# Attention and expert layer on one core: query rows repeated by zero-step DRAM reads, and batch 0's queries cut 512 + 288 + 288, the last two among the expert work

## The chip, the cores and the metric

The kernel runs on one core of one Trainium2 chip. The metric is the device time of one execution in microseconds (us), the median of the runs. A profile of one more execution gives the trace: every instruction of every engine with its start and duration, what it waited for, and the DMA packets. The engines are TensorE (PE; its weight loads have a row of their own, PEld), VectorE (DVE), ScalarE (ACT), GpSimd (POOL) and SyncE (SP), which here only issues DMA transfers. Each runs its own instructions in order and waits for others by semaphores.

## The reference, cut to what matters

```python
# attention: q, k, v are (4, 4, 1088, 32); S1, S2 are (8, 32), float64
def phi(x):                                   # 64 features of a row
    a = np.einsum('rd,bhsd->bhsr', S1, x)
    b = np.einsum('rd,bhsd->bhsr', S2, x)
    return np.einsum('bhsi,bhsj->bhsij', a, b).reshape(*x.shape[:-1], 64)
q_p, k_p = phi(q), phi(k)
kv = np.einsum('bhsf,bhsd->bhfd', k_p, v)
z = np.sum(k_p, axis=2)
x = num / den       # num = q_p kv, den = q_p z + 1e-6; then (4352, 128)

# routed experts: w_gate (128, 8), w1 (8, 128, 1024), w2 (8, 1024, 128)
P = np.exp(x @ w_gate - max)                  # then 8 rounds of row and
out = 0                                       # column normalisation
for e in range(8):
    out += P[:, e:e+1] * (np.maximum(x @ w1[e], 0) @ w2[e])
```

## The kernel before, in words

All arithmetic is in 32-bit floats. Nearly all of the time is the experts' two matrix products. They are cut into *steps* of a generator, `steps()`: one step is the first product of 128 hidden units with one tile of tokens (`first`, L894, two matmuls of 64 output rows each, side by side in the array), its ReLU on ScalarE (L898), and those second products (`into`, L1067) and VectorE sums (L911, L956) that have come due. `fill(n)` runs about `n` / share steps, where a step of 256 tokens counts as 0.53. The attention is written as short pieces with `fill` between them, so that TensorE has expert work while VectorE and ScalarE prepare the next piece. The order on PE and DVE, and in the opening part on ACT too, is the order of the program; the issuing order of DMA transfers and of GpSimd's work is left to a scheduler.

The experts without a weight (`groups`, the first ones of expert 0) need only `xT`, the attention's result transposed, so they can begin when the first tokens of batch 0 are done. PSUM has eight banks: four of the tag `a`, handed out in turn by `bank()`, for everything that is read soon, and four (`s0` to `s3`) for the experts' sums. A new use of a bank waits until its last reader is done.

Batch 0 goes a way of its own, because nothing can hide it:

- 15 matmuls on a tile of ones (L114) run while the first loads arrive. `projections` turns the float64 S1 and S2 to 32 bits and writes the block weights `wd` (one block a head).
- `transpose_k`, `keys_ab` (L304): keys turned, and their two projections `a` and `b` made for all heads.
- `keys_products` (L320), `keys_sums` (L336), `keys_kept`: products a_i b_j of the keys, their sums with v, and the copy of these to `kvz`.
- `query_products(c)` (L366) for three chunks of queries: 384, 352 and 352. The weights `wq` hold each row of S1 and S2 repeated, so that one matmul gives a_i for all 64 pairs (i, j) of two heads and the other gives b_j; the contraction is over the 64 rows of two heads, and the two head pairs run side by side as row tiles. The results lie in `s0` to `s3`. ScalarE copies the a part (L369), `multiply` (L375) forms the product on VectorE.
- `fractions(c)` (L384) makes numerators and denominators, `divide(c)` (L396 to L403) turns the denominators, takes reciprocals, turns them back and writes `xT`.

Batches 1 to 3 make a and b once (`queries_ab`, L419, weights `wdq`), store them to DRAM and read them back with each row repeated over partitions: `qa` is stored with every element twice and read in four transfers to `ph` (`repeat_a`, L435), `qb` is stored eightfold and read in one transfer to `rb` (`repeat_b`, L438). VectorE multiplies `ph` by `rb` in thirds (`times`, L445), `tops` (L454) forms numerators and denominators, `over` (L467 to L473) divides. `take_over` sends the result through DRAM to `xT`. `attention(b)` holds these pieces, with a `fill(1.4)` after each.

Of the kernel before, what the change touches and what calls it, by code (L numbers as in the profile page):

```python
# [10 lines left out]
F32 = mybir.dt.float32  # L11
U32 = mybir.dt.uint32
Act = mybir.ActivationFunctionType
Alu = mybir.AluOpType
# [36 lines left out]
def kernel(  # L51
# [49 lines left out]
    for n, (s, queue) in enumerate(((S1, nc.sync), (S2, nc.scalar))):  # L101
        queue.dma_start(out=raw[:, n], in_=s.bitcast(U32).unsqueeze(0).to_broadcast([P // R, R, words * D]))
# [10 lines left out]
    for _ in range(15):  # L113
        nc.tensor.matmul(warm[:, 0:P], ones, ones, start=True, stop=True)  # L114
# [49 lines left out]
    def load_q(b):  # L164
        qx = ld.tile([P, SA, D], F32, tag="q", name="qx")
        nc.sync.dma_start(out=qx, in_=q[b].rearrange("h (s a) d -> (h s) a d", a=SA))
        loaded["q", b] = qx
# [13 lines left out]
    load_q(0)  # L181
    load_v(0)
    load_q(1)

# [65 lines left out]
    wdq = consts.tile([P, 2, H * R], F32, name="wdq")  # L250
# [10 lines left out]
    def repeated(st):  # L261
        for s in range(2):
            one = half[:, s:s + 1].unsqueeze(2).to_broadcast([P, R, R])
            nc.vector.tensor_tensor(wq[:, 0, s], st[:, 0, 0:R].unsqueeze(2).to_broadcast([P, R, R]), one, op=Alu.mult)
            nc.vector.tensor_tensor(wq[:, 1, s], st[:, 1, 0:R].unsqueeze(1).to_broadcast([P, R, R]), one,
                                    op=Alu.mult)


        nc.gpsimd.tensor_copy(wdq[:, 0], wd[:, 0].rearrange("p h r -> p (h r)"))
        nc.gpsimd.tensor_copy(wdq[:, 1].rearrange("p (r h) -> p r h", h=H), wd[:, 1].rearrange("p h r -> p r h"))  # L270
# [11 lines left out]
    load_v(1)  # L282
# [8 lines left out]
    def transpose_k(b):  # L291
        kx = loaded["k", b]
        nc.vector.transpose(out=kT[:, 0:NT * P].rearrange("p (t c s) -> p c t s", c=4, s=32),  # L293
                            in_=kx[:, 0:4 * NT, :].rearrange("p (c t) d -> p c t d", c=4))
        nc.vector.transpose(out=kT[:, NT * P:S], in_=kx[:, 4 * NT:SA, :].rearrange("p a d -> p (a d)"))

    def keys_ab(b):

        ab = wk.tile([P, 2, NT + 1, H * R], F32, tag="ab", name="ab", bufs=1)
        pk = bank().rearrange("p (t n f) -> p t n f", t=NT, n=2)  # L300
        for t in range(NT):
            for s in range(2):
                sl = slice(64 * s, 64 * (s + 1))
                nc.tensor.matmul(pk[sl, t].rearrange("p n f -> p (n f)"), kT[:, P * t + 64 * s:P * t + 64 * (s + 1)],  # L304
                                 wdf, start=True, stop=True, tile_position=(0, 64 * s))
        nc.scalar.copy(ab[:, :, 0:NT, :], pk.rearrange("p t n f -> p n t f"))
        pr = bank()[0:64, 0:2 * H * R]
        nc.tensor.matmul(pr, kT[:, NT * P:S], wdf, start=True, stop=True, tile_position=(0, 0))
        nc.scalar.copy(ab[0:64, :, NT, :], pr.rearrange("p (n f) -> p n f", n=2))
        keys[b] = ab  # L310
# [32 lines left out]
    def keys_kept(b):  # L343
        pv = sums_of.pop(b)
        for s in range(2):
            sl = slice(64 * s, 64 * (s + 1))
            if b:
                x, y = kvs[b % 2][sl, :, s, :], pv[sl].rearrange("p i c d -> p i (c d)")[:, :, 0:D + 1]
            else:
                x, y = kvz[sl, :, :, s, :], pv[sl].rearrange("p i c d -> p c i d")  # L350
            if s:
                nc.vector.tensor_copy(x, y)
            else:
                nc.scalar.copy(x, y)

    chunks = ((0, 384), (384, 736), (736, S))

    def query_products(c):

        lo, hi = chunks[c]  # L360
        n = hi - lo
        banks = [[mps.tile([P, 512], F32, tag=f"s{2 * i + m}", name="s") for m in range(2)] for i in range(2)]
        for m in range(2):
            for i in range(2):
                sl = slice(64 * i, 64 * (i + 1))
                nc.tensor.matmul(banks[i][m][:, 0:n], wqf[sl, m, :], qT[sl, lo:hi], start=True, stop=True,  # L366
                                 tile_position=(64 * i, 0))
        for i in range(2):
            nc.scalar.copy(phs[0][:, i, lo:hi], banks[i][0][:, 0:n])  # L369
        queries[0, c] = [banks[i][1][:, 0:n] for i in range(2)]  # L370

    def multiply(c):
        lo, hi = chunks[c]
        for i, pb in enumerate(queries[0, c]):
            nc.vector.tensor_tensor(phs[0][:, i, lo:hi], phs[0][:, i, lo:hi], pb, op=Alu.mult)  # L375

    def fractions(c):

        lo, hi = chunks[c]
        n = hi - lo  # L380
        pn, pd = bank(), bank()
        for t, m in ((pd, 1), (pn, 0)):
            for i in range(2):
                nc.tensor.matmul(t[64 * i:64 * (i + 1), 0:n], kvz[:, m, i].rearrange("p h d -> p (h d)"),  # L384
                                 phs[0][:, i, lo:hi], start=True, stop=True, tile_position=(0, 64 * i))
        queries[0, c] = pn, pd

    def divide(c):


        lo, hi = chunks[c]
        n = hi - lo
        nb = n // 32
        pn, pd = queries.pop((0, c))
        rd = wk.tile([P, 384], F32, tag="rd", name="rd")
        nc.vector.transpose(out=rd[:, 0:n], in_=pd[:, 0:n])  # L396
        rc = wk.tile([P, 12], F32, tag="rc", name="rc")[:, 0:nb]
        nc.vector.tensor_scalar_add(rc, rd[:, 0:n].rearrange("p (b r) -> p b r", r=32)[:, :, 0], 1e-6)
        nc.vector.reciprocal(rc, rc)
        rd = wk.tile([P, 384], F32, tag="rd", name="rd")  # L400
        nc.vector.transpose(out=rd[:, 0:n].rearrange("p (b r) -> p b r", r=32),
                            in_=rc.unsqueeze(2).to_broadcast([P, nb, 32]))
        nc.vector.tensor_tensor(xT[:, lo:hi], pn[:, 0:n], rd[:, 0:n], op=Alu.mult)  # L403
# [6 lines left out]
    def queries_ab(b):  # L410
        qa = dram.tile([H * R, 2, 2, 2 * W9], F32, name=f"qa{b}")
        qb = dram.tile([2, R, 2 * R, 2, 2 * W9], F32, name=f"qb{b}")
        ab = wk.tile([P, 3, 192], F32, tag="qab", name="qab", bufs=1)
        x = (kT if b == 1 else qT).rearrange("p (h q c t s) -> p h c t q s", h=2, q=2, c=3, t=3)
        for cs in ((0, 1), (2,)):
            pq = bank()[:, 0:192 * len(cs)].rearrange("p (c n) -> p c n", n=192)
            for i, c in enumerate(cs):
                for s in range(2):
                    nc.tensor.matmul(pq[64 * s:64 * (s + 1), i].rearrange("p (t q s) -> p t q s", t=3, q=2),  # L419
                                     wdq.rearrange("p n f -> p (n f)"), x[:, s, c], start=True, stop=True,  # L420
                                     tile_position=(0, 64 * s))
            nc.scalar.copy(ab[:, cs[0]:cs[-1] + 1], pq)
        abf = ab.rearrange("p c n -> p (c n)")
        for s in range(2):
            x = abf[64 * s:64 * s + 32].unsqueeze(1).to_broadcast([32, 2, 2 * W9])
            nc.sync.dma_start(out=qa[:, :, s], in_=x)
        for s in range(2):
            for h in range(2):
                x = abf[64 * s + 32 + h:64 * (s + 1):2].unsqueeze(1).to_broadcast([2 * R, R, 2 * W9])
                nc.sync.dma_start(out=qb[h, :, :, s].rearrange("i f n -> f i n"), in_=x)  # L430
        queries[b] = qa, qb

    def repeat_a(b):
        for j in range(4):
            nc.sync.dma_start(out=phs[b % 2][j::4], in_=queries[b][0].rearrange("(x r) j s n -> (r j) x (s n)", x=2))  # L435

    def repeat_b(b):
        nc.sync.dma_start(out=rb, in_=queries.pop(b)[1].rearrange("h i (j x) s n -> (h i j) x (s n)", x=2))  # L438
# [25 lines left out]
    def over(b, c):  # L464
        pn = queries.pop((b, c))
        rc = wk.tile([P, 12], F32, tag="rc", name="rc").rearrange("p (t h) -> p t h", h=H)
        nc.vector.reciprocal(rc, pn[:, :, :, D])  # L467
        xs = wk.tile([P, 384], F32, tag="rd", name="rd").rearrange("p (h t d) -> p h t d", h=H, t=3)
# [671 lines left out]
    with tc.manual_schedule(engines={engines.DVE, engines.PE, engines.Activation}):  # L1140
        st = projections()
        transpose_k(0)
        keys_ab(0)
        repeated(st)
        load_k(1)
        transpose_q(0, 0, chunks[0][1])
        query_products(0)
# [3 lines left out]
        multiply(0)  # L1151
        transpose_q(0, chunks[0][1])
        keys_kept(0)
        transpose_q(1)
        query_products(1)
        fractions(0)
        multiply(1)
        queries_ab(1)
        load_q(2)
# [3 lines left out]
        fractions(1)  # L1163
        query_products(2)
        divide(1)
    with tc.manual_schedule(engines={engines.DVE, engines.PE}):
        fill(1)
        multiply(2)
        fractions(2)
        fill(1)  # L1170
        transpose_k(1)
        load_k(2)
        load_v(2)
        load_q(3)
        divide(2)
        fill(1.5)
        keys_ab(1)
        fill(1)
        keys_products(1, 0)
        fill(1)  # L1180
        keys_products(1, 1)
        fill(1)
        keys_products(1, 2)
        fill(1)
# [41 lines left out]
```

## Time and profile before

| | |
|---|---|
| time, median of 3 runs | 932.12 us (931.32 to 932.35) |
| span of the profiled execution | 929.5 us |
| TensorE matmuls busy | 915.1 us, 98% |
| VectorE busy | 696.7 us, 75% |
| ScalarE busy | 417.5 us, 45% |
| GpSimd busy | 204.3 us, 22% |
| DMA | 128.14 MB, 138 GB/s in the mean |

The page gives for each engine its busy time, then a row of 40 equal slices of the span (23 us each), in which a digit is the busy share in tenths. A line of the order of time gives the start, the duration, the engine, the line of the kernel, the operation, its output and inputs, the number of merged instructions, and in brackets the idle time before it with what ended it. A 32-bit matmul appears as two records (two passes). A busy TensorE is one that has matmuls under way, not one at its peak.

### The profile page before, as it was taken

The numbers are of one execution on the slowest core, as the hardware profiler recorded it, in microseconds if no ns is written. First come the engines' busy times: TensorE is split into PE (matmuls) and PEld (weight loads), VectorE is DVE, ScalarE is ACT, GpSimd is POOL, SyncE is SP. The second block draws the span as 40 slices with busy tenths as digits, with TensorE's granted clock in tenths as the row PEclk, the third lists the DMA queues.
The fourth block names the chain that finished last, engine by engine and source line by source line (L and its number), as shares of the span: only waits on it lengthen the run. The fifth ranks groups of instructions, "written<-read, shape, count | busy, mean of one in ns | idle before, by whom it ended". The sixth has DMA issues, their size and how long they took to land.

```text
span 929.5 us, 18877 instructions
## 1 busy us (share of the span) xinstructions
PE 915.1 (98%) x7434; PEld 596.6 (64%) x7434; DVE 696.7 (75%) x1200; ACT 417.5 (45%) x901; POOL 204.3 (22%) x198
## 2 busy tenths in 40 slices
PE   9999999999999999999999999999999999999997
PEld 6667544568888888875555555555555555556886
DVE  8787789896779788686976666965757977768665
ACT  2445345654444454444544444544445444445443
POOL 2021100172545502030020101101110343310220
PEclk9999999999999999999999999999999999999999
DMA  9987100222345535353444434363434555553650
GB/s 229 288 250 218 52 1 1 80 98 63 109 153 170 171 118 155 115 195 118 136 136 143 159 113 143 113 189 125 146 111 154 150 151 184 171 179 91 173 152 12
DMA packets 91640, 128.14 MB, mean 138 GB/s; under 512 B 25376, under 2 KB 69488, under 8 KB 86816
## 3 DMA queue, kind: packets, MB, share of 16 engines
q1 hardware_dynamic: 89344, 123.63, 42.9%
q0 software_dynamic: 976, 3.15, 1.1%
q8 instruction: 58, 0.95, 0.4%
q10 hardware_dynamic: 1232, 0.16, 0.1%
q14 instruction: 30, 0.25, 0.1%
HBM read 107.88 MB, written 19.05 MB: 137 GB/s over the span
## 4 chain that ended last, share of the span: by engine, by line
PE 91%; DVE 6%; issue 1%; ACT 1%; DMA 0%; SPq 0%; POOL 0%; DVEq 0%; ACTq 0%; POOLq 0%
PE a L894 49%; PE s L1067 39%; DVE hb L911 1%; PE a L336 1%; PE a L114 1%; DVE hb L956 1%; PE a L454 1%; DMA ph<-qa 0%; PE a L304 0%; ACT hb L898 0%; DVE cs L593 0%; DVE kp L320 0%; DVE kT L293 0%; DVE pqg L956 0%; PE a L488 0%
## 5 line engine op out<-in xcount | busy, mean ns | idle before, releaser
L894 PE MATMUL a<-xe,w 128*64 128x256 f32 (+1 forms) x2560 | 571.3, 470 | 0.0
L898 ACT ACTIVATE hb<-a 128x256 f32<-128x256 f32 (+4 forms) x408 | 195.3, 480 | 253.4 <-PE a L894 226.3
L894 PEld LDWEIGHTS a<-xe,w 128*64 128x64 f32 x2560 | 242.7, 137 | 76.6 <-issue 1.6
L1067 PE MATMUL s<-hb,ws 128*64 128x256 f32 (+3 forms) x1344 | 267.5, 395 | 1.8 <-DVE w L723 0.9
L898 ACT ACTIVATE hx<-a 128x256 f32<-128x256 f32 (+1 forms) x360 | 167.3, 465 | 214.5 <-PE a L894 194.7
L1067 PE MATMUL s<-hx,ws 128*64 128x256 f32 x1280 | 235.4, 379 | 0.0
L956 DVE TENSOR_TENSOR hb<-hb 128x512 f32<-128x512 f32 (+1 forms) x204 | 133.8, 666 | 95.2 <-ACT hb L898 90.3
L956 DVE TENSOR_TENSOR hx<-hx 128x512 f32<-128x512 f32 (+1 forms) x204 | 148.8, 739 | 68.0 <-ACT hx L898 63.1
L663 POOL TENSOR_TENSOR xe<-xT,xe 128x768 f32<-128x768 f32 (+2 forms) x41 | 84.8, 2070 | 501.7 <-DMA xe<-pT 405.4
L1067 PEld LDWEIGHTS s<-hb,ws 128*64 128x64 f32 x1344 | 127.8, 137 | 92.7 <-issue 63.8
L1067 PEld LDWEIGHTS s<-hx,ws 128*64 128x64 f32 x1280 | 121.2, 137 | 78.7 <-issue 59.4
L894 PE MATMUL a<-xT,w 128*64 128x416 f32 (+3 forms) x512 | 124.4, 464 | 1.3 <-DVE rd L469 0.9
L1067 PE MATMUL s<-hb,w 128*64 128x256 f32 (+3 forms) x496 | 109.6, 410 | 0.5 <-DVE kept L723 0.4
L911 DVE TENSOR_TENSOR hb<-hb 128x416 f32<-128x416 f32 (+7 forms) x96 | 68.1, 711 | 18.2 <-ACT hb L898 12.9
L1067 PE MATMUL s<-hx,w 128*64 128x256 f32 x384 | 76.5, 379 | 0.0
L894 PEld LDWEIGHTS a<-xT,w 128*64 128x64 f32 x512 | 51.8, 137 | 28.7 <-issue 11.8
L1067 PEld LDWEIGHTS s<-hb,w 128*64 128x64 f32 x496 | 50.0, 137 | 23.2 <-issue 6.8
L239 POOL TENSOR_TENSOR ws<-w 128x256 f32<-128x256 f32 (+1 forms) x70 | 59.4, 883 | 12.8 <-PE a L894 9.8
L911 DVE TENSOR_TENSOR hx<-hx 128x256 f32<-128x256 f32 (+1 forms) x65 | 38.8, 602 | 24.6 <-ACT hx L898 20.8
L956 DVE TENSOR_TENSOR pqg<-hb 128x512 f32<-128x512 f32 x68 | 47.5, 739 | 0.0
L1067 PEld LDWEIGHTS s<-hx,w 128*64 128x64 f32 x384 | 38.6, 137 | 8.5
L956 DVE TENSOR_TENSOR pqg<-hx 128x512 f32<-128x512 f32 x68 | 36.4, 574 | 0.0
(170 smaller groups left out, 477.6 us busy)
## 6 DMA issues: line engine op xcount, KB each, us to landing
w<-in_moe_w_dram SPq DMA_DIRECT2D x82, 512.0 KB, 5.6
ws<-ws SPq DMA_DIRECT2D x34, 1024.0 KB, 5.0
xe<-pT SPq DMA_DIRECT2D x34, 384.0 KB, 4.1
ws<-ws SPq DMA_DIRECT2D x12, 512.0 KB, 3.7
qb<-qab SPq DMA_DIRECT2D x12, 288.0 KB, 5.2
ph<-qa SPq DMA_DIRECT2D x12, 288.0 KB, 4.7
rb<-qb SPq DMA_DIRECT2D x3, 1152.0 KB
pb<-pT SPq DMA_DIRECT2D x6, 384.0 KB, 7.4
```

The lines of the kernel that those rows point to most:

```text
L114: nc.tensor.matmul(warm[:, 0:P], ones, ones, start=True, stop=True)
L239: tc.keep_in_program_order(nc.gpsimd.tensor_tensor(ws[:, c:c + len(ns)], blocks(x), blocks(y), op=Alu.subtract if off else Alu.add))
L336: nc.tensor.matmul(pv[64 * s:64 * (s + 1), i], kp[0:n, H * t + h].rearrange("p i j -> p (i j)"), vx[0:n, slots[h], t, :], start=(t == 0 an ...
L454: nc.tensor.matmul(pn[64 * s:64 * (s + 1), t, 2 * i:2 * i + 2].rearrange("p h d -> p (h d)"), ph[:, i, s, 64 * t:64 * (t + 1)], kvs[b % 2] ...
L663: tc.keep_in_program_order(nc.gpsimd.tensor_tensor(out, x, pb, op=Alu.mult))
L894: nc.tensor.matmul(ph[sl], loaded_w[j][0][:, P * f + H2 * s:P * f + H2 * (s + 1)], sources[j][:, lo:hi], start=True, stop=True, tile_posit ...
L898: nc.scalar.activation(out=out, in_=ph, func=Act.Relu)
L911: nc.vector.tensor_tensor(out, a, b, op=Alu.subtract)
L956: nc.vector.tensor_tensor(out if not isinstance(out, tuple) else places(*out), places(*a), places(*b) if isinstance(b, tuple) else b, op=A ...
L1067: nc.tensor.matmul(sums[g][i][H2 * s:H2 * (s + 1), n * place:n * (place + 1)], w, x, start=c == 1, stop=c == per, tile_position=(0, H2 * s))
```

## The change

It has two aims. The first is to move less through DRAM for batches 1 to 3: a and b are stored once, 16 rows by 2304 numbers each, and the repeats are made by the reading side with a step of zero; with that `wdq` isn't needed any more. The half of `rb` for the upper 64 partitions is issued by GpSimd. The second is to let the first expert work begin after one chunk of 512 queries, and to make the products of the other two chunks (288 each) among the expert steps. For that these two use `a` banks and weights `wz`, which hold zeros outside one head and contract over all 128 rows, one matmul a head, side by side as column tiles like the experts' own. Around it: S1 and S2 come by the queues of ScalarE and GpSimd, so that the keys are SyncE's first load; `wq` and `wz` are written by GpSimd; batch 0's keys go in two halves; 14 warming matmuls and not 15; both copies to `kvz` on ScalarE; and the loads and fills in a new order.

```diff
-    for n, (s, queue) in enumerate(((S1, nc.sync), (S2, nc.scalar))):
+    for n, (s, queue) in enumerate(((S1, nc.scalar), (S2, nc.gpsimd))):
...
-    for _ in range(15):
+    for _ in range(14):
...
     load_k(0)
-    load_q(0)
+    load_q(0, 0, 16)
     load_v(0)
     load_q(1)
+    load_q(0, 16)
...
     def repeated(st):
+        def repeat(out, column):
+            one = column.unsqueeze(2).to_broadcast([P, R, R])
+            nc.gpsimd.tensor_tensor(out[:, 0], st[:, 0, 0:R].unsqueeze(2).to_broadcast([P, R, R]), one, op=Alu.mult)
+            nc.gpsimd.tensor_tensor(out[:, 1], st[:, 1, 0:R].unsqueeze(1).to_broadcast([P, R, R]), one, op=Alu.mult)
...
+            repeat(wq[:, :, s], half[:, s:s + 1])
+        for h in range(H):
+            repeat(wz[:, :, h], own[:, h:h + 1])
...
-            if s:
+            if s and b:
                 nc.vector.tensor_copy(x, y)
...
-    chunks = ((0, 384), (384, 736), (736, S))
+    chunks = ((0, 512), (512, 800), (800, S))
...
+        else:
+            banks = {i: [bank(), bank()]}
+            for m in range(2):
+                for s in range(2):
+                    nc.tensor.matmul(banks[i][m][64 * s:64 * (s + 1), 0:n],
+                                     wz[:, m, 2 * i + s].rearrange("p i j -> p (i j)"), qT[:, lo:hi],
+                                     start=True, stop=True, tile_position=(0, 64 * s))
...
     def queries_ab(b):
-        qa = dram.tile([H * R, 2, 2, 2 * W9], F32, name=f"qa{b}")
-        qb = dram.tile([2, R, 2 * R, 2, 2 * W9], F32, name=f"qb{b}")
+        ds = [dram.tile([2 * R, 2, 2, 2 * W9], F32, name=f"q{n}{b}") for n in "ab"]
...
-        for s in range(2):
-            x = abf[64 * s:64 * s + 32].unsqueeze(1).to_broadcast([32, 2, 2 * W9])
-            nc.sync.dma_start(out=qa[:, :, s], in_=x)
-        for s in range(2):
-            for h in range(2):
-                x = abf[64 * s + 32 + h:64 * (s + 1):2].unsqueeze(1).to_broadcast([2 * R, R, 2 * W9])
-                nc.sync.dma_start(out=qb[h, :, :, s].rearrange("i f n -> f i n"), in_=x)
+        for s in range(2):
+            for n, d in enumerate(ds):
+                lo = 64 * s + 32 * n
+                nc.sync.dma_start(out=d[:, :, s].rearrange("r x n -> x r n"), in_=abf[lo:lo + 32])
...
     def repeat_a(b):
-        for j in range(4):
-            nc.sync.dma_start(out=phs[b % 2][j::4], in_=queries[b][0].rearrange("(x r) j s n -> (r j) x (s n)", x=2))
+        rows = queries[b][0].rearrange("r x s n -> r (x s n)")
+        nc.sync.dma_start(out=phs[b % 2], in_=rows.unsqueeze(1).to_broadcast([2 * R, R, 8 * W9]))
     def repeat_b(b):
-        nc.sync.dma_start(out=rb, in_=queries.pop(b)[1].rearrange("h i (j x) s n -> (h i j) x (s n)", x=2))
+        rows = queries.pop(b)[1].rearrange("r x s n -> r (x s n)")
+        for h, queue in enumerate((nc.sync, nc.gpsimd)):
+            queue.dma_start(out=rb[64 * h:64 * (h + 1)],
+                            in_=rows[R * h:R * (h + 1)].unsqueeze(0).to_broadcast([R, R, 8 * W9]))
```

The opening order after the change stands below. Before, the products of all three chunks and two of the three `divide`s stood ahead of the first `fill`, and the fills up to `attention(1)` came to n = 7.5; now they come to 6.25.

```python
projections, repeated, transpose_k(0) in halves, keys_ab(0) in halves
transpose_q(0, 0:512), query_products(0), keys_products(0), keys_sums(0)
multiply(0), keys_kept(0), transpose_q(1), fractions(0, denominators)
queries_ab(1), fractions(0, numerators), repeat_a(1), repeat_b(1)
divide(0), transpose_q(0, 512:1088)
fill(0.5), query_products(1, heads 0 and 1), fill(0.5), multiply
query_products(1, heads 2 and 3), fill(0.5), multiply, fill(0.5)
transpose_k(1), fractions(1), fill(0.5), query_products(2, heads 0 and 1)
divide(1), fill(0.5), multiply, query_products(2, heads 2 and 3)
fill(0.5), multiply, keys_ab(1), fill(0.5), fractions(2)
keys_products(1, 0), fill(0.75), divide(2), keys_products(1, 1), fill(0.75)
keys_products(1, 2), fill(0.75), then attention(1)
```

## The prediction, made before the changed kernel ran

> **What bounds the kernel now.** I read the page's busy rows first, then the waits and the order of time of the first 40 us, where every edit lies.
>
> ```profile
> PE 915.1 (98%) x7434; PEld 596.6 (64%) x7434; DVE 696.7 (75%) x1200; ACT 417.5 (45%) x901; POOL 204.3 (22%) x198
> PE   9999999999999999999999999999999999999997
> DMA  9987100222345535353444434363434555553650
> ```
>
> TensorE (PE) is busy in all 40 slices; the DMA row is full only in the first three. So an edit is worth what it does to TensorE's own work and to its pauses. I split the span that way. One expert step (two matmuls of 256 columns, four records in the trace) takes 0.43 us in the chain of waits wherever it runs freely, that is 0.84 ns for a column of a pair of passes that run side by side. All matmuls at this rate come to 902 us. The other 27 us are lost: 6.9 before the first expert matmul at 20.0, 9.3 by the end of batch 1's key sums at 35.1, about 19 by 110 us, only 2.5 in the 820 us after that, and some 6 at the end. The change can win back a part of the first 19 us and nothing else.
>
> The order of time of the start (start, duration, then the instructions):
>
> ```profile
> 1.00 6.31 PE L114 MATMUL a<-ones 128*128 128x128 f32 x30 [1.00 <-POOL own L116]
> 3.39 0.20 DVE L34 TENSOR_SCALAR mant<-raw 128x64 uint32<-128x64 uint32 x1 [1.64 <-DMA raw<-in_S_dram]
> 7.25 1.15 PE L304 MATMUL a<-wd,kT 128*64 128x64 f32 x32
> 8.49 1.56 PE L366 MATMUL s<-qT,wq 64*128 64x384 f32 x8
> 9.06 2.69 DVE L320 TENSOR_TENSOR kp<-ab 128x1024 f32<-128x1024 f32 x3 [0.63 <-ACT ab L306]
> 10.35 2.66 PE L336 MATMUL a<-v,kp 128*64 128x64 f32 x72 [0.30 <-DVE kp L320]
> 13.65 1.46 PE L366 MATMUL s<-qT,wq 64*128 64x352 f32 x8 [0.64 <-DVE qT L289]
> 15.03 1.51 PE L384 MATMUL a<-ph,kvz 128*64 128x384 f32 x8
> 16.07 0.58 DVE L396 STREAM_TRANSPOSE rd<-a 128x384 f32<-128x384 f32 x1
> 17.99 0.56 DVE L403 TENSOR_TENSOR xT<-a,rd 128x384 f32<-128x384 f32 x1
> 20.02 0.65 PE L894 MATMUL a<-xT,w 128*64 128x256 f32 x4
> ```
>
> The warm-up matmuls (L114) cost 0.21 us a record, twice the later rate. The attention of batch 0 is a ping-pong of TensorE, VectorE (DVE) and ScalarE (ACT), with a pause of 0.3 to 0.8 us at each turn. Two waits of the stretch that follows matter:
>
> ```profile
> DVE ph L445 <- DMA rb<-qb: 1.7, 1, 1.7
> PE a L454 <- DVE rd L469: 0.8, 1, 0.8
> ```
>
> The first is VectorE waiting for batch 1's repeated `b` rows until 34.9 us; the second is TensorE waiting for VectorE to free a PSUM bank at 42.8.
>
> [...] L366's records start in pairs 7 to 40 ns apart[...]. [...] records 0.21 us apart until 6.7 us, 0.11 from there. [...] The new stores are 2x16x576 from 32 partitions[...]; each half of the new `rb` read has outermost sizes 64 and 8[...]. No view of before shows a transfer of that kind.[...]
>
> **The change part by part.**
>
> 1. *Query products.* Before: four matmuls a chunk, four pairs of passes, over 1088 columns in all: 4 x 1088 x 0.84 ns = 3.7 us. After: 4 x 512 columns as before, then eight pairs over 576 columns: 1.7 + 3.9 = 5.6 us. This adds **1.9 us** to a full TensorE. Nothing hides it.
>
> 2. *S1 and S2 on the ACT and GpSimd queues, 14 warm-ups.* The first key load moves from 1.5 to 0.7 us and lands about 0.8 us sooner, at 5.1. S2 is generated by GpSimd: before's GpSimd issues take 0.55 to 0.73 us and land in 2.4 to 3.0 when little else is queued, so S2 lands at 3.1 to 3.7 (3.3 before), I take 3.5. The issue holds up GpSimd's memset of `ones`, for which the warm-up waits: it starts at about 1.6 instead of 1.0, and 14 x 0.43 us end at 7.6 (7.3 before). The keys are turned from 5.9 as before. So the start of real work is **0.3 us later**.
>
> 3. *Keys in two halves, wq on GpSimd, 512 first queries.* The key projections run 7.6 to 8.7; the first half is copied out by ScalarE at 8.6, and the products (2.69 us) run 8.6 to 11.3 instead of 9.06 to 11.7. TensorE does the 512-column query products to 10.6 (1.72 us) and the key sums to 12.8 (13.0 before). The 12 small GpSimd products (0.2 to 0.3 us each) lie beside this. Then: both `kvz` copies on ScalarE, 0.26 us each, to 13.4; denominators to 14.3; batch 1's projections (L419's 1.0 us) to 15.3; numerators to 16.2. `divide` takes 2.48 us for 384 columns (16.07 to 18.55); three of its passes grow by 0.19 us with 512, so 3.05: 14.4 to 17.45. The first expert matmul starts at **17.5**, after a pause of 1.3 us. TensorE has by then lost 7.2 us, against 6.9 at 20.0 before. It comes earlier because it has done less, not because it waited less.
>
> 4. *Chunks 1 and 2 among the expert work.* From 17.5 I carried each instruction in its engine's order with before's durations (expert step 0.43; L366's work now 0.97 a head pair; `multiply` 0.43; `divide` of 288 columns 1.85; key transposes 1.4). There are four `a` banks, taken in turn. So the second product of chunk 2 waits for chunk 1's denominators to be turned (0.3 us); the next expert step waits for the numerators' bank, which `divide(1)` frees at 25.0 behind the 1.4 us key transposes on VectorE (0.9 us); the one after `divide(2)` waits 0.5 us; and the first wait for `qT` is 0.3. That is some 2 us, and before lost 2.4 between 20.0 and 35.1. Key sums of batch 1 end at 35.35 (before 35.12), with two expert steps and three second products fewer done: 2 x 0.43 + 3 x 0.215 = 1.5. TensorE is **1.7 us behind** there.
>
> 5. *DRAM reads with zero steps.* A batch wrote 288 + 1152 KB and read 2304 KB; it now writes 288 KB and reads 2304. Four stores replace six and two reads (three issues) replace five, so the SyncE queue gets free sooner. Against that stand the two engines: 16 packets of 2304 bytes a store and engine, 64 in all. Before's packets of this size took 93 ns at the fast end and 158 in the mean, so 6 to 10 us. Issued from 15.9, after the key load that lands near 18, the last store lands at 24 to 28.5 (26.6 before). Behind it on SyncE wait the repeats, then batch 2's queries and keys, which have over 6 us to spare; on GpSimd the half of `rb` holds up the weight sums of expert 1, wanted only after 60 us. `rb` lands at 31 to 34.5; VectorE wants it at 34.8. I take it as hidden: the 1.7 us wait goes, but VectorE gets there no sooner, because two of the three `divide`s of batch 0 now run after 22 us and not one. In batches 2 and 3 `rb` landed 1.3 and 4.4 us before its use; nothing waits and nothing is won.
>
> 6. *Attention of batch 1.* More expert matmuls now stand between its top products (three steps, not two, before the second), so the 1.0 us TensorE pause at 42.8 shrinks to 0.3: **0.7 us back**. The rest is the same code with the same fill.
>
> Sum: +1.7 - 0.7 = about +1.0 us, **933.0** for 932.12, which is within 0.2% (1.86 us) of before.
>
> **Rivals.** *A, slower:* the stores on two engines are at the slow end and queue behind the loads, so that `rb` comes at 37.5 and VectorE, and with it TensorE's top products, stand 2 to 3 us; a late S2 adds up to 0.5. For it: the DMA row is full in this stretch, and the margin is 0.3 us at the slow end. Against: expert work fills TensorE while VectorE waits. 933.0 + 2.5 = 935.5. *B, faster:* VectorE, which runs without idle time from 45 to 63 us in before, is what makes TensorE pause by about 5 us between 50 and 96. Freed of four `wq` products, one copy and the `rb` wait it could be 1 to 1.5 us ahead, and each of some four pauses of 0.7 to 1.1 us shrinks by that; with the bank waits of step 4 hidden too, the time is 933.0 - 4 = 929. Against: my order gives it no lead at 35 us.[...]
>
> **How the numbers follow.** Forecast 0.40: my sum is small against its own error, which I put at 2 us (five waits of 0.3 to 1 us each guessed to half their size, and the two unknown transfers). A has 0.34: the added 1.9 us is certain, what pays it back is not. B has 0.26. The range, 929.2 to 936.2, takes in B's whole time and A's[...]. The chances of faster, same and slower are the cases' own.
>
> **What would show it.** Right: the new query products about 1.94 us a chunk in TensorE's record; first expert matmul at 17 to 18 us; the wait for `rb` gone; `divide(1)` named as releaser of an expert step near 25 us; landings of the stores above 5 us. Wrong: TensorE's loss by 35 us under 8 us (B), or VectorE waiting for `rb` by over 1 us in any batch (A). A matmul rate of the new products away from 0.84 ns a column would void step 1.

## The result, and the profile after

| | before | after |
|---|---|---|
| time, median | 931.72 us | 947.39 us (946.92 to 948.51) |
| ratio, 95% interval | | 1.0172 (1.0154 to 1.0189) |
| span of the profiled execution | 929.5 us | 946.0 us |
| DMA bytes | 128.14 MB | 124.60 MB |

The change costs 15.7 us; 933.0 was forecast, with a range that ended at 936.2. The busy row of the engines and three rows of the 40 slices, from the page of the changed kernel:

```profile
PE 919.9 (97%) x7448; PEld 568.6 (60%) x7448; DVE 694.1 (73%) x1196; ACT 418.2 (44%) x903; POOL 208.5 (22%) x212
PE   8699999999999999999999999999999999999997
PEclk9889999999999999999999999999999999999999
DMA  6857210032343355453544343444343565452650
```

TensorE's row has one hole, the 6 in the second slice (24 to 47 us); before, that slice had a 9. The DMA row fell from 9987 to 6857 in the first four slices. Fewer bytes have to move, and yet the DMA engines got less done while the kernel was waiting for them.

The order of time of the opening, changed kernel (start, duration, instruction, idle time before it):

```profile
2.26 6.21 PE L114 MATMUL a<-ones 128*128 128x128 f32 x28 [2.26 <-POOL own L116]
5.63 0.20 DVE L34 TENSOR_SCALAR mant<-raw 128x64 uint32<-128x64 uint32 x1 [3.88 <-DMA raw<-in_S_dram]
8.78 1.28 PE L311 MATMUL a<-wd,kT 128*64 128x64 f32 x32 [0.31 <-DVE kT L299]
15.20 1.08 PE L399 MATMUL a<-ph,kvz 128*64 128x512 f32 x4 [0.63 <-ACT kvz L362]
18.42 0.69 DVE L417 TENSOR_TENSOR xT<-a,rd 128x512 f32<-128x512 f32 x1
19.16 0.65 PE L908 MATMUL a<-xT,w 128*64 128x256 f32 x4 [1.06 <-DVE xT L417]
```

VectorE has S1 and S2 at 5.63 us and not at 3.39, the key projections (L311; L304 before) begin at 8.78 and not at 7.25, and the first expert matmul at 19.16. Then the hole. Lines of the waits (total, times, longest, in us):

```profile
DVE ph L459 <- DMA rb<-qb: 15.7, 2, 10.3
PE a L468 <- DVE kvs L360: 10.7, 1, 10.7
```

And the order of time where it ends:

```profile
46.02 0.96 DVE L459 TENSOR_TENSOR ph<-ph,rb 128x768 f32<-128x768 f32 x1 [10.34 <-DMA rb<-qb]
46.89 1.60 DVE L925 TENSOR_TENSOR hb<-hb 128x512 f32<-128x512 f32 x3
48.52 0.23 DVE L360 COPY kvs<-a 64x66 f32<-64x66 f32 x1
48.81 1.59 PE L468 MATMUL a<-kvs,ph 128*64 128x66 f32 x24 [10.72 <-DVE kvs L360]
50.37 1.10 PE L908 MATMUL a<-xT,w 128*64 128x256 f32 x4
51.25 1.07 PE L1081 MATMUL s<-hb,ws 128*64 128x256 f32 x4
```

Read from above: VectorE stands 10.34 us at `times(1, 0)`, because the repeated `b` rows land at 45.3 and 45.9 us (34.9 before). Behind it in VectorE's order wait three expert sums and the copy of `kvs`; the top products (L468) want `kvs`; and all of TensorE's expert work stands behind the top products. So a wait that TensorE has no part in stops it for 10.72 us. The last two lines show a second price: eight records take from 50.37 to 52.32 us, 0.24 us each, against 0.11 when TensorE runs on; the clock granted between 48 and 52 us was 0.50. Batch 2 repeats it smaller: the second of the two `rb` waits is 5.3 us, and TensorE pauses 2.3 us before its top products at 82.3.

Split as the prediction splits the span, with its rate a column unrounded: matmul work 903.7 us (901.9 before), TensorE's start 1.26 us later, loss after that 33.8 us (20.3 before), and some 6 us at the end in both. 1.8 + 1.3 + 13.5 = 16.6, and the spans differ by 16.5.

### The profile page after: what moved, and what is told of

Read it like the earlier page. It is cut to its first block, busy times and chain, and to the rows that moved or that the text cites. A ratio compares the mean times of both kernels' runs of the same rounds, so it can differ in the third digit from the quotient of the medians.

```text
span 946.0 us, 18902 instructions
## 1 busy us (share of the span) xinstructions
PE 919.9 (97%) x7448; PEld 568.6 (60%) x7448; DVE 694.1 (73%) x1196; ACT 418.2 (44%) x903; POOL 208.5 (22%) x212
## 2 busy tenths in 40 slices
DMA packets 89560, 124.60 MB, mean 132 GB/s; under 512 B 25072, under 2 KB 69184, under 8 KB 84352
## 4 chain that ended last, share of the span: by engine, by line
PE 88%; DVE 6%; DMA 3%; issue 1%; ACT 1%; SPq 0%; DVEq 0%; ACTq 0%; POOLq 0%
PE a L908 48%; PE s L1081 37%; DMA rb<-qb 2%; DVE hb L925 2%; DMA qb<-qab 1%; PE a L344 1%; DVE hb L970 1%; PE a L468 1%; DMA raw<-in_S_dram 0%; DVE kT L299 0%; DVE rd L483 0%; PE a L502 0%; PE a L311 0%; DVE pqg L970 0%; PE s L376 0%
## 5 line engine op out<-in xcount | busy, mean ns | idle before, releaser
L908 PEld LDWEIGHTS a<-xe,w 128*64 128x64 f32 x2560 | 239.7, 137 | 91.8 <-issue 1.8
L1081 PEld LDWEIGHTS s<-hb,ws 128*64 128x64 f32 x1344 | 125.2, 137 | 99.6 <-issue 58.7
L925 DVE TENSOR_TENSOR hx<-hx 128x256 f32<-128x256 f32 (+1 forms) x65 | 39.6, 614 | 23.9 <-ACT hx L912 22.8
L970 DVE TENSOR_TENSOR pqg<-hb 128x512 f32<-128x512 f32 x68 | 45.1, 703 | 0.0
```

Of the source, the lines that this page charges most:

```text
L908: nc.tensor.matmul(ph[sl], loaded_w[j][0][:, P * f + H2 * s:P * f + H2 * (s + 1)], sources[j][:, lo:hi], start=True, stop=True, tile_posit ...
L925: nc.vector.tensor_tensor(out, a, b, op=Alu.subtract)
L970: nc.vector.tensor_tensor(out if not isinstance(out, tuple) else places(*out), places(*a), places(*b) if isinstance(b, tuple) else b, op=A ...
L1081: nc.tensor.matmul(sums[g][i][H2 * s:H2 * (s + 1), n * place:n * (place + 1)], w, x, start=c == 1, stop=c == per, tile_position=(0, H2 * s))
```

## The experiments

Each was timed beside the kernel before on the same chip, and the ratios are to that. In the first four, D stands for "the new DMA scheme makes the rows late", with D1, the stores on two engines (between 57 and 63 us of the changed kernel, when batch 2's stores moved nearly alone, 12.8% of the 16 engines' time was busy, two engines' worth); D2, the repeating reads; D3, batch 1's values queued between; and F for "the new opening and the products among the expert work".

**The DMA scheme alone, and all but the DMA scheme.** e1 is the kernel before with the stores, reads and weights of the changed `queries_ab`, `repeat_a`, `repeat_b`. e2 is the changed kernel with those of before.

> The kernel before with the new stores and zero-step reads alone. Theory D (the time went into the DMA path: the rows of batches 1 to 3 arrive late): rb of batch 1 lands at 38 to 44 us instead of 34.9, VectorE waits for it by 5 us or more, 936 to 944 us. Theory F (the time went into the new opening and the query products among the expert work): no wait for rb above 2 us, 930 to 933 us.

> The changed kernel with the stores and reads of before. Theory D: no long wait for rb, and what remains is the added 1.9 us of query products less what the opening saves, 931 to 935 us. Theory F: the loss stays, 942 to 948 us.

e1: 945.45 us, ratio 1.0144 (1.0128 to 1.0159). `rb` lands at 45.0 us, and the wait is the changed kernel's:

```profile
DVE ph L442 <- DMA rb<-qb: 19.3, 2, 11.8
```

e2: 938.57 us, 1.0069 (1.0054 to 1.0084). So the DMA scheme is most of it, by more than D had allowed (944), and the rest of the change is not innocent either: e2 lies between the two theories, and its `rb` landed at 39.2 us with the old scheme too. The two parts add to 2.1%, more than the 1.7% of the whole, so they overlap.

**The stores.** e3 cuts each store of the changed kernel by 16 rows, so that 16 is the outermost size of both sides; e4 loads batch 1's values before the stores.

```diff
# e3, in queries_ab
-                lo = 64 * s + 32 * n
-                nc.sync.dma_start(out=d[:, :, s].rearrange("r x n -> x r n"), in_=abf[lo:lo + 32])
+                for x in range(2):
+                    lo = 64 * s + 32 * n + 16 * x
+                    nc.sync.dma_start(out=d[:, x, s], in_=abf[lo:lo + 16])
# e4
     first_w = load_w(0)
+    load_v(1)
     load_k(1)
...
         fractions(0, 0)
-        load_v(1)
```

> The changed kernel with each of the four stores cut in two by 16 rows, so that 16 is the outermost size of both sides. If the two-engine stores are the cause (D1), the last store lands about 5 us earlier (22 instead of 27 us), rb follows by as much, 940 to 943 us. If the repeating reads are the cause (D2), the stores land early all the same and rb gains 2 us or less, 945 to 948 us.

> The changed kernel with v of batch 1 loaded ahead of the stores as in the kernel before, so that its 0.54 MB are not in the queue with the repeats. If the queue order is the cause (D3), rb of batch 1 lands 3 us earlier or more and 943 us or less; if not, 946 to 948 us.

e3: 953.84 us, 1.0235 (1.022 to 1.025). The stores were done by 22.8 us and not 27.2, and SyncE's half of `rb` landed at 45.2 all the same. D1 falls. The time missed D2's 945 to 948 as well: in batch 2 GpSimd issued its half of `rb` at 76.7 us, 16 us after SyncE's and 10.6 later than in the changed kernel, and VectorE waited 12.0 us for it, not 5.3. That is read from the trace; no run undid it alone. e4: 947.27 us, 1.0174 (1.015 to 1.0198), `rb` at 43.6, 2.3 us sooner and not 3, and no gain in time: D3 falls for the changed kernel. What is left is D2, the reads.

**Which read.** f1 is the kernel before with the new store and read of `a` alone, f2 with those of `b` alone (and the weights `wd`). Of each only the store is printed; the read is that of the change.

```diff
# f1
-            x = abf[64 * s:64 * s + 32].unsqueeze(1).to_broadcast([32, 2, 2 * W9])
-            nc.sync.dma_start(out=qa[:, :, s], in_=x)
+            nc.sync.dma_start(out=qa[:, :, s].rearrange("r x n -> x r n"), in_=abf[64 * s:64 * s + 32])
# f2
+            nc.sync.dma_start(out=qb[:, :, s].rearrange("r x n -> x r n"), in_=abf[lo:lo + 32])
```

> Kernel before, with only the `a` rows changed: 16 rows stored once per quarter and read by one zero-step read (`ph`), the `b` rows as before. Theory Rb (the read of `b` is what is late: its two halves share eight engines and read 147 KB each over and over): `ph` takes 12 us as in the changed kernel but is wanted late, `rb` keeps its distinct rows and lands by 37, time 931 to 935. Theory Ra (the read of `a` is as slow and stands ahead of `rb` in the engines): `rb` lands after 40 us in batch 1, VectorE waits over 5 us, time 938 or more.

> Kernel before, with only the `b` rows changed: 16 rows stored once, read by two zero-step halves on the SyncE and GpSimd queues; `ph` by its four reads as before. Theory Rb: `rb` lands after 42 us in batch 1, VectorE waits 8 us or more, time 940 to 946. Theory Ra: `rb` lands by 38, time 931 to 936.

f1: 936.72 us, 1.0056 (1.0039 to 1.0072); `ph` took 11.4 us from issue to landing (5.0 to 5.5 for each of before's four), and `rb`, though stored as of old, came at 40.9 behind it. f2: 942.35 us, 1.0123 (1.0108 to 1.0138), `rb` at 42.4. Both reads are slow; Ra and Rb each had half, and f1's time lies between theirs.

**Why a read is slow.** These runs vary one property of a read each. f3 is e1 with rows 68 KB apart, i1 is f1 with rows 36 KB apart; g5 is f1 with eight plain reads in place of one with a zero step; g4 is f1 with four copies of `a` in DRAM.

```diff
# f3
+        ds = [dram.tile([2 * R, 17408], F32, name=f"q{n}{b}")[:, 0:8 * W9].rearrange("r (x s n) -> r x s n", x=2, s=2) for n in "ab"]
# i1
+        qa = dram.tile([2 * R, 4, 2, 2, 2 * W9], F32, name=f"qa{b}")[:, 0]
# g5
-        nc.sync.dma_start(out=phs[b % 2], in_=rows.unsqueeze(1).to_broadcast([2 * R, R, 8 * W9]))
+        for j in range(R):
+            nc.sync.dma_start(out=phs[b % 2][j::R], in_=rows)
# g4
...
+        rows = queries[b][0].rearrange("r c x s n -> (r c) (x s n)")
+        nc.sync.dma_start(out=phs[b % 2], in_=rows.unsqueeze(1).to_broadcast([8 * R, 2, 8 * W9]))
```

> The kernel with the DMA edits alone (945.45 us), with each DRAM row 68 KB from the next, so that the same bytes are read from a region 7.5 times as wide. Theory H (many engines reading one small piece of DRAM get in each other's way): packets of 9216 bytes take near 350 ns at full rate, `rb` lands by 37, time 931 to 936. Theory Z (the zero steps, their eight engines or their queue are slow in themselves): `rb` lands after 42 as before this edit, time 943 to 947.

> The kernel of f1 (936.72 us) with `a` stored in four copies (576 KB in place of 147) and read by one transfer with a zero step of two. Theory H (the rate falls with the number of different bytes that are read): packets of 9216 bytes in `ph` take 350 to 480 ns, `ph` takes 6 to 9 us. Theory Z (a zero step is slow in itself): they take 600 to 750 ns as in f1.

> The kernel of f1 with the one zero-step read of `a` replaced by eight plain reads of the same 16 rows, no zero step anywhere. Theory H: packets of 9216 bytes take 600 to 750 ns as in f1, time 935 or more. Theory Z: they take 350 to 450 ns, `rb` lands by 37, time 931 to 934.

> The kernel of f1 (936.72 us): `a` stored once, 147 KB, read by one transfer with a zero step of eight, but its 16 rows 36 KB apart in DRAM instead of 9 KB[...]. Theory H (few different bytes are slow): packets of 9216 bytes in `ph` take 600 to 740 ns as in f1, time 935 to 938. Theory A (the distance between the rows that are read at one moment makes them slow): they take 350 to 420 ns, `rb` lands by 37, time 931 to 934.

And three undo the few bytes, but keep other properties. h_eight is the kernel before with its `b` rows all distinct as of old, one row of padding after every eight, read in two halves as in the changed kernel. i2 pads by eight rows. k1 joins the halves of h_eight to one read:

```diff
# h_eight
+        qb = dram.tile([2, R, R + 1, 2, 2, 2 * W9], F32, name=f"qb{b}")[:, :, 0:R]
...
+        for h, queue in enumerate((nc.sync, nc.gpsimd)):
+            queue.dma_start(out=rb[64 * h:64 * (h + 1)], in_=rows[h])
# k1: rows as "(h i) j (x s n)"
+        nc.sync.dma_start(out=rb, in_=rows)
```

> The kernel before, its `b` rows all distinct in DRAM as they were (1152 KB), but padded and read in two halves, each with an outermost size of 8, on the SyncE and GpSimd queues as in the changed kernel. Theory E (eight engines, not the few bytes, make `rb` slow): packets of 9216 bytes near 350 ns on half of the engines, `rb` lands at 38 to 42, time 934 to 940. Theory H (the few bytes alone): both halves land by 36, time 931 to 932.5.

> The kernel of h_eight (960.32 us), its eight groups of `b` rows 144 KB apart in DRAM instead of 81 KB. Theory E (eight engines alone): packets of 9216 bytes in `rb` of batch 3, which runs alone, take 500 to 715 ns as in h_eight, time 958 to 963. Theory A (the distance): they take 350 to 400 ns there, and the time falls below 957.

> The kernel of h_eight (960.32 us), with its two half reads joined to one on the SyncE queue, outermost size 16, from the same padded rows 81 KB apart: only the split into halves over eight engines is undone. Theory E (the split makes the `b` rows late): packets of 9216 bytes take 347 to 400 ns, `rb` of batch 1 lands by 36, time 930 to 933. Theory L (the padded layout in DRAM makes them slow): packets take 500 ns or more, `rb` lands after 38, time 935 or more.

Theory H falls with h_eight, but E did not foresee it either: packets of 581 ns for its 350, and 960 us for its 934 to 940. i2 came out as h_eight had. k1, where E had full speed back, is slow too: 935.11 us, `rb` at 39.2, as its theory L had it.

The DMA view of a stretch in which almost nothing but the repeating read moves gives the mean time of a packet of 9216 bytes: share x 16 engines x stretch / such packets. First the kernel before (`rb`, 31.5 to 34 us):

```profile
DMA packets 116, 1.02 MB, mean 409 GB/s; under 512 B 4, under 2 KB 4, under 8 KB 6
q1 hardware_dynamic: 116, 1.02, 97.6%
```

0.976 x 16 x 2.5 us / 110 = 355 ns. Then f1 (`ph`, 31 to 36 us):

```profile
DMA packets 134, 1.11 MB, mean 221 GB/s; under 512 B 14, under 2 KB 14, under 8 KB 14
q1 hardware_dynamic: 134, 1.11, 98.0%
```

0.98 x 16 x 5 us / 120 = 653 ns: all engines busy at half the rate. g4 (`ph`, 31.5 to 35 us):

```profile
DMA packets 177, 1.47 MB, mean 420 GB/s; under 512 B 17, under 2 KB 17, under 8 KB 18
q1 hardware_dynamic: 177, 1.47, 100.1%
```

k1 (`rb`, 32 to 36 us):

```profile
DMA packets 102, 0.86 MB, mean 214 GB/s; under 512 B 6, under 2 KB 6, under 8 KB 12
q1 hardware_dynamic: 102, 0.86, 97.1%
```

h_eight (`rb` of batch 3, its SyncE half alone, 98 to 102 us):

```profile
DMA packets 57, 0.53 MB, mean 131 GB/s; under 512 B 0, under 2 KB 0, under 8 KB 0
q1 hardware_dynamic: 57, 0.53, 51.2%
```

And the changed kernel (`rb` of batch 3, both halves, 95 to 99 us):

```profile
DMA packets 96, 0.89 MB, mean 223 GB/s; under 512 B 0, under 2 KB 0, under 8 KB 0
q0 software_dynamic: 48, 0.44, 26.2%
q1 hardware_dynamic: 47, 0.43, 25.7%
```

The medians from the packet records of these stretches (31 to 36 us for g5 and i1, 27 to 32 for f3, 99 to 102 for i2), by the outermost size of the read's DRAM side, that is the number of groups of partitions that one read is cut into:

| read | outermost | different bytes | packet | GB/s | ratio |
|---|---|---|---|---|---|
| before, `rb` | 128 | 1152 KB | 347 ns | 409 | 1 |
| g4, `ph`, zero step of 2 | 64 | 576 KB | 347 ns | 420 | 1.0017 (1.0009 to 1.0024) |
| f1, `ph`, zero step of 8 | 16 | 144 KB | 656 ns | 221 | 1.0056 |
| g5, `ph`, no zero step | 16 | 144 KB | 622 ns | 202 | 1.0064 (1.0042 to 1.0087) |
| i1, `ph`, rows 36 KB apart | 16 | 144 KB | 650 ns | 222 | 1.0054 (1.0037 to 1.0071) |
| f3, `ph`, rows 68 KB apart | 16 | 144 KB | 685 ns | 229 | 1.0165 (1.0149 to 1.018) |
| k1, `rb`, padded | 16 | 1152 KB | 685 ns | 214 | 1.0057 (1.0039 to 1.0075) |
| h_eight, half of `rb` | 8 | 2 x 576 KB | 581 ns | 131 | 1.031 (1.0285 to 1.0335) |
| i2, half of `rb` | 8 | 2 x 576 KB | 607 ns | 135 | 1.0309 (1.0294 to 1.0325) |

What falls: the zero step (g5 has none and is as slow, g4 has one and is fast); the distance of the rows in DRAM (i1, f3, i2); and the theory that f1, g4 and g5 had seemed to bear out, few different bytes, since k1 reads 1152 different KB at half rate. Nor is padding in DRAM, which L blamed, needed: f1 and g5 have none and are as slow (656 and 622 ns, 685 in k1). What all nine agree on is the outermost size: 64 and 128 are fast, 16 and 8 are slow. Before's four `ph` reads add 32 to the fast side: between 28.5 and 31 us their packets of 4608 bytes took 178 ns, half of 347, at 387 GB/s. k1 against before is the cleanest pair, with the same bytes and queue, all engines busy in both (97.1 and 97.6%), and one row of padding that keeps the sixteen groups from joining to 128 rows.

The changed kernel's own `rb` stands apart: its packets take 348 ns, as in before, and 52% of the engines' time is busy. Eight engines at that speed move 8 x 9216 / 348 ns = 212 GB/s, so there the half rate needs no cause but half the engines.

Why the packets of a read in few groups are slow was not shown. Two kinds of plain read also differ in the partitions they write: each of g5's eight reads writes 16 partitions that lie 8 apart, with packets of 622 ns and 202 GB/s; each of before's four `ph` reads writes 32 that lie 4 apart, at 387 GB/s. No run changed the partitions or their order alone, and that 64 groups are as fast as 128 rests on g4 alone.

h_eight and i2 lose more than 1.4% for another reason too: GpSimd issued its half of batch 2's `rb` at 77.6 us, 16 us after SyncE's, behind its other work.

**The rest of the change.** f4 is the changed kernel with the DMA scheme of before, batch 1's values loaded before the stores, and S1 and S2 on their old queues with 15 warm-ups. g1 is f4 with the new S queues and 14 warm-ups, g2 is f4 with the values loaded late.

```diff
# g1, against f4
-    for n, (s, queue) in enumerate(((S1, nc.sync), (S2, nc.scalar))):
+    for n, (s, queue) in enumerate(((S1, nc.scalar), (S2, nc.gpsimd))):
# g2, against f4
-    load_v(1)
     load_k(1)
...
         fractions(0, 0)
+        load_v(1)
```

> The changed kernel with the DMA scheme of before, batch 1's values loaded before the stores, and S1 and S2 on the SyncE and ScalarE queues with 15 warm-ups: what is left of the change is the new order of the work and the query products over 128 rows. Theory Q (the added 1.9 us of query products and nothing else remains): first expert matmul at 17.0 to 18.0, time 932 to 935. Theory F (the interleaved order itself makes pauses): key sums of batch 1 end after 36.5, time 936 or more.

> The kernel of f4 (931.95 us) with S1 and S2 on the ScalarE and GpSimd queues and 14 warm-ups, as in the changed kernel. Theory S (the late S2 is worth what it delays): TensorE's start and first expert matmul 1.2 to 1.5 us later than in f4 (17.63 us), time 933 to 934. Theory N (the pause is made up for by ScalarE and VectorE, which then have work waiting): 931.5 to 932.5.

> The kernel of f4 with batch 1's values loaded where the changed kernel loads them, behind the stores and ahead of the repeats. Theory V (six value loads and their queue stand ahead of `ph` and `rb`): `rb` lands after 38 us, VectorE waits for it 3 to 4 us, time 935.5 to 938. Theory N (the loads only trade places): `rb` lands by 36, time 931.5 to 932.5.

f4: 931.95 us, ratio 1.0007 (1.0001 to 1.0014). Its order of time:

```profile
17.63 0.65 PE L912 MATMUL a<-xT,w 128*64 128x256 f32 x4 [1.05 <-DVE xT L421]
25.38 0.71 PE L386 MATMUL a<-qT,xt 128*64 128x288 f32 x4 [0.49 <-ACT hb L916]
26.59 0.71 PE L386 MATMUL a<-qT,xt 128*64 128x288 f32 x4 [0.50 <-ACT ph L390]
28.21 1.15 PE L315 MATMUL a<-wd,kT 128*64 128x64 f32 x32 [0.49 <-ACT hb L916]
```

g1: 934.2 us, 1.0032 (1.0021 to 1.0044): S2's transfer, issued by GpSimd at 1.3 us in the changed kernel, lands at 5.6, and the memset for the warm-ups stands behind the issue. Theory S, a little above its size. S1, now on ScalarE's queue, is later too, 4.5 us for 3.3 before; the key load that now goes ahead of both may have a part, and no run separates the two. g2: 933.99 us, 1.0028 (1.0013 to 1.0042), `rb` at 37.5, a wait of 3.4 us. The wait is theory V's, but the landing is before its 38 us and the time below its 935.5. Both edits together are e2, whose 0.69% is near the 0.53% that f4 and the two add up to.

**A version that beats both.** g3 is f4 with the later chunks' products over 64 rows again: first both head pairs' `a` factors, side by side as row tiles in two `a` banks, then both `b` factors. g7 also moves batch 1's key transposes behind `divide(1)`.

```diff
# g3, c > 0; i is now the factor, not the head pair
+            pair = [bank(), bank()]
+            for j in range(2):
+                sl = slice(64 * j, 64 * (j + 1))
+                nc.tensor.matmul(pair[j][:, 0:n], wqf[sl, i, :], qT[sl, lo:hi], start=True, stop=True,
+                                 tile_position=(64 * j, 0))
# g7, against g3
-        transpose_k(1)
-        load_k(2)
         fractions(1, 1)
         fractions(1, 0)
+        divide(1)
         fill(0.5)
         query_products(2, 0)
-        divide(1)
+        transpose_k(1)
+        load_k(2)
```

> The kernel of f4 (931.95 us, 1.0007 of before), with the query products of the later chunks over 64 rows again, a pair of row tiles side by side, two banks at a time: all numerator factors first, then all second factors. Theory Q (the 1.9 us of added matmul work is all that f4 pays): TensorE's own work 901.9 us as before, its loss some 19 us, ratio 0.998 to 0.9995. Theory W (the wait for banks and for ScalarE's copies grows by what the work shrinks): ratio 1.000 to 1.002.

> The kernel of g3 with batch 1's key transposes (1.4 us of VectorE) moved behind the division of chunk 1, which frees two PSUM banks. Theory Q with the bank waits of f4 at 25.4, 26.6 and 28.2 us (0.66 us each) cut by half: 0.5 to 1 us faster than g3. Theory W (those waits end at ScalarE's copies, not at the division): within 0.3 us of g3.

g3: 930.06 us, 0.9985 (0.9978 to 0.9992). Matmul work 901.9 us as before, loss 19.4 (20.3 before). This is 1.9 us under f4, which is what the 128-row products add. g7: 930.09 us, 0.999 (0.9981 to 1.0); as W said, the division was not what TensorE waited for.

## Why the prediction was wrong

- **Step 5 failed.** It priced the new stores ("the last store lands at 24 to 28.5"; 27.2 measured), and gave the reads the old rate: "`rb` lands at 31 to 34.5 ... I take it as hidden". `rb` landed at 45.9. From the last store to `rb` the step allowed 6 to 7 us, before took 8.3, and 18.7 were measured. The step counted the stores' engines (two, as measured), but did not ask what rate a read in 16 or 8 groups has. A half of `rb` alone kept 51.2% of the engines' time busy (h_eight), both halves together 52%, and no view of before could show that `ph`, with all engines busy (98.0% in f1), runs at half rate too. At the 221 and 223 GB/s measured, a 1152 KB read takes 5.3 us and not 2.9, and two follow each other in every batch, beside loads that share the engines. "In batches 2 and 3 ... nothing waits" failed with it: batch 2 waits 5.3 us. e1 shows the size of this alone, 1.44%.
- **Step 5 also left out** that `load_v(1)` moves behind the stores, ahead of both repeats. It does nothing in the changed kernel (e4), but costs 0.2% where the reads are quick (g2 against f4).
- **Step 2 was mis-sized.** S2 "I take 3.5" landed at 5.6; warm-up 1.6 was 2.26; "0.3 us later" was 1.5 (8.78 for 7.25). g1 against f4 gives the price of the new queues: 0.25%, or 2.3 us.
- **Step 3 was right in itself.** The first expert matmul, forecast at 17.5, stood at 19.16; with the S queues undone f4 has it at 17.63, after a pause of 1.05 us (1.3 forecast).
- **Step 1 was right.** Work rose from 901.9 to 903.7 us, and g3 wins back 1.9 us.
- **Steps 4 and 6, in f4,** gave the sum by errors that cancel. Key sums of batch 1 ended at 36.9 us (35.35 forecast). TensorE was 1.9 us of work and 1.6 us of loss (9.9 for 8.3, from its start) behind, together 3.5 and not 1.7. The bank waits were there and near the forecast sum, but ScalarE ended them (`hb` L916, `ph` L390 above), not `divide(1)`. Then 3.1 us came back and not 0.7: before's pauses at 42.8, 53.9 and 68.2 us are gone or smaller. f4's +0.07% is the forecast's +0.1%, by luck.
- **Rival A** had the mechanism, `rb` late, with 2 to 3 us for a pause of 10.7. It put the lateness down to the stores, and "expert work fills TensorE while VectorE waits" was the wrong comfort: that work stood behind the top products in TensorE's own order.

## What to carry to other kernels

Price a transfer by its access pattern and not by its bytes: a version that moves 3% fewer bytes was slower because its reads are cut into 8 or 16 groups of partitions (131 to 229 GB/s measured here) where the old ones were cut into 32 or 128 (387 and 409). Before counting a DMA wait as hidden, list what stands behind the waiting instruction on its engine, and what stands behind that on TensorE, and ask what happens if it comes 10 us late. When a change has many parts and the whole is slow, undo each part by itself; here the part that was right, the new order with 512 queries first and the rest among the expert work, gains 0.15% once the DMA scheme, the S queues, the late values and the 128-row products are undone (g3).

## What the runs showed of the hardware

- Reads of 9216 bytes a partition took 347 ns a packet and moved 409 to 420 GB/s with an outermost size of 128 or 64, and 622 to 685 ns and 202 to 229 GB/s with 16, the DMA engines being some 90% busy or more in both.
- The time of a packet doesn't tell the rate by itself: in the changed kernel's `rb` of batch 3 a packet took 348 ns, as in before, but only 52% of the engines' time was busy, and 223 GB/s moved.
- The load of S2 took 4.3 us to land when GpSimd issued it behind the key load, and 2.1 when ScalarE issued it at the start (before).
- After 10.7 us without work TensorE ran eight records at 0.24 us each, under a granted clock of 0.50, before it was back at 0.11 under 1.00 (52.6 to 56 us).
